# Attention beside a two-layer product on one core: half-array matmuls issued in longer rows, and one PSUM pool of four banks

## The chip, the cores and the metric

The kernel runs on one core of a Trainium2 chip. The metric is the device time of one execution in microseconds; the time before is the median of three runs, 242.66 us (242.25 to 243.97). Everything below that is read from a profile is read from one profiled execution of the kernel before.

## The reference

For each of 4 batches and 8 heads, 768 queries of 64 numbers attend to the keys within 15 places of their own (a band of 31) and, beside them, to one summary per block of 32 tokens: the maximum of the block's keys, with the mean of its values, and log 32 added to the score. The result, 3072 rows of 512, goes through two products with a quick GELU between them.

```python
k_sum = k.reshape(B, H, nb, block, D).max(axis=3)
v_sum = v.reshape(B, H, nb, block, D).mean(axis=3)
mask_l = np.abs(pos[:, None] - pos[None, :]) < window
scores_all = np.concatenate([where(mask_l, scale*q@k.T, -1e9), scale*q@k_sum.T + log(block)], axis=-1)
attn = softmax(scores_all) @ np.concatenate([v, v_sum], axis=2)
h = x @ w_in                      # x: attn as 3072 x 512
out = (h * sigmoid(1.702 * h)) @ w_out
```

## The kernel before

The work is cut into eight **units** u = 0 to 7, half a batch each (384 rows of x). A unit has two stages on TensorE (PE). `ff_in` makes the hidden layer: 16 groups (nt) of four matmuls `ph` of 384 columns, each group followed by a GELU on ScalarE (ACT). `ff_out` makes the output: three row blocks (ms) of 16 matmuls `po` of 512 columns, cut into 12 **slots** of four matmuls each. In u = 0 the slots run over the three blocks in turn, so three `po` tiles are open at once; in the other units one block is done before the next.

The attention of unit u+1 is woven between the slots of unit u, by a table `plan` (L705) that the function `beside` (L708) reads after each slot. For each of four head pairs p it has three steps:

- `s<p>`, `scores` (L470): twelve matmuls `ps_s` of 64 columns that use 64 of the array's 128 rows; then the exponential on ACT and the mask multiply on VectorE (DVE). The first exponential of a unit stands behind a load of ACT's table.
- `v<p>`, `values` (L487): twelve matmuls `ps_av` of 65 columns that use 64 of the array's 128 columns, for the two heads, three query blocks and two halves. Of the 65 columns 64 are the sums and one is the weights' total. `norm` (L501) is a reciprocal and a multiply on DVE and leaves `x_sb`.
- `x<p>`, `tx` (L508): three full-array transposes `ps_x` of `x_sb`, and a DVE copy to `xT[p]`, which the matmul number p of each `ph` group of the next unit reads.

The engines do their instructions in the order in which the program issues them (`_Ordered`, L17, whose helper line L27 all rows of the profile carry). So an instruction that waits holds all that stands behind it on its engine.

When a batch has ended (u = 1, 3 and 5), the next batch's keys, values and queries are prepared within `ff_in`: GpSimd (POOL) casts them; PE transposes keys (`tk`, L454) after groups 1, 2, 4 and 6, block sums of values (`vsum`, L235) after groups 8 and 9, queries (`tq`, L464) after groups 10, 11, 13 and 14. Behind each `tk` stands a chain on DVE: a copy out of PSUM, a maximum `ks` over blocks, and five small copies; behind the second half of `vsum` four small casts `vs`, from which two DMAs on the SP queue fill the summary rows of `vw` (`vrows`, L286) that the first `v` of the next unit reads.

PSUM has eight banks, in three pools: `psb` (two tiles of two banks: scores, values, transposed keys and queries), `psx` (one bank: `ps_x` and the block sums `ps_vs`) and `pmm` (three banks: `ph`, `po`). A tile must wait until the last reader of the earlier tile in its banks is done.

Of the kernel before, what the change touches and what calls it, by code (L numbers as in the profile page):

```python
# [9 lines left out]
F32 = mybir.dt.float32  # L10
BF16 = mybir.dt.bfloat16
# [23 lines left out]
def kernel(  # L35
# [10 lines left out]
    B, H, S, D = q.shape  # L46
# [5 lines left out]
    NP = H // 2  # L52
# [17 lines left out]
    keep = ctx.enter_context(tc.tile_pool(name="keep", bufs=1))  # L70
# [2 lines left out]
    attp = ctx.enter_context(tc.tile_pool(name="att", bufs=4))  # L73
    outp = ctx.enter_context(tc.tile_pool(name="outp", bufs=3))
    psb = ctx.enter_context(tc.tile_pool(name="psb", bufs=2, space=bass.MemoryType.PSUM))
    psx = ctx.enter_context(tc.tile_pool(name="psx", bufs=1, space=bass.MemoryType.PSUM))
    pmm = ctx.enter_context(tc.tile_pool(name="pmm", bufs=3, space=bass.MemoryType.PSUM))

# [88 lines left out]
    vs = keep.tile([128, H, VC], BF16, name="vs")  # L167
    vse = keep.tile([128, H, VC], BF16, name="vse")
    vso = keep.tile([128, H, VC], BF16, name="vso")
    xT = [keep.tile([128, HALF], BF16, name=f"xT{p}") for p in range(NP)]  # L170
    gT = [keep.tile([128, NT, HALF], BF16, name=f"gT{s}") for s in range(2)]
    w_in_sb = keep.tile([128, KO, d_ff], BF16, name="w_in_sb")
    w_out_sb = keep.tile([128, NT, d_model], BF16, name="w_out_sb")
# [59 lines left out]
    vs_ps = [None]  # L233

    def vsum(s, js):  # L235

        if js[0] == 0:
            vs_ps[0] = psx.tile([128, 2 * D], F32, name="ps_vs", tag="x")
        w5 = vw[s].rearrange("p (j e) h c -> p j e h c", e=2)
        for j in js:  # L240
            o = 20 - 4 * j
            for g in range(4):
                pe.matmul(out=vs_ps[0][32 * g:32 * g + 32, :], lhsT=E[:, o:o + 32],
                          rhs=w5[:, j, 0, 2 * g:2 * g + 2, 0:D],
                          start=(j == 0), stop=(j == NJ - 1), skip_group_check=True)
# [132 lines left out]
    def v_sum(j):  # L378

        if j == 0:  # L380
            st["VS"] = psx.tile([128, H * D], F32, name="ps_vs", tag="x")
# [46 lines left out]

    def x_turn(p):
        src = x_sb.pop(p)  # L430
        pool_, tag = (psx, "x") if st["nx"] % 2 == 0 else (pmm, "mm")
        st["nx"] += 1
        st["X", p] = pool_.tile([128, HALF], BF16, name="ps_x", tag=tag)
# [36 lines left out]
    def scores(b, half, p):  # L470

        a = a_sb[p] = attp.tile([128, 2, TH, QT], BF16, name="a_sb", tag="a_sb")
        big = psb.tile([128, 1024], F32, name="ps_s", tag="big")
        for i in range(TH):
            t = half * TH + i
            for h in range(2):
                r = slice(h * 64, h * 64 + 64)
                pe.matmul(out=big[:, h * 512 + i * QT:h * 512 + i * QT + QT],
                          lhsT=kx[p][b % 2][r, t, :], rhs=qT[p][r, t * QT:t * QT + QT],
                          start=True, stop=True)  # L480
        act.activation(out=a.rearrange("p h t c -> p h (t c)"),
                       in_=big.rearrange("p (h c) -> p h c", h=2)[:, :, 0:HALF],
                       func=ACT.Exp, scale=scale)
        dve.tensor_mul(a, a, mk[:, half * TH:(half + 1) * TH, :].unsqueeze(1)
                       .to_broadcast([128, 2, TH, QT]))

    def values(b, half, p):  # L487

        a = a_sb[p]
        big = psb.tile([128, 1024], F32, name="ps_av", tag="big")  # L490
        pv = big[:, 0:390].rearrange("p (h j c) -> p h j c", h=2, j=JH)
        for hh in range(2):
            for j in range(JH):
                for e in range(2):
                    t = 2 * j + e
                    pe.matmul(out=pv[e * 64:e * 64 + 64, hh, j, :], lhsT=a[:, hh, t, :],
                              rhs=vw[b % 2][:, half * TH + t, 2 * p + hh, 0:D + 1],
                              start=True, stop=True, skip_group_check=True)
        norm(p, pv)

    def norm(p, pv):  # L501
        rc = attp.tile([128, 2, JH, 1], F32, name="rc", tag="rc")
        dve.reciprocal(out=rc, in_=pv[..., D:D + 1])
        x_sb[p] = attp.tile([128, JH, 2, D], BF16, name="x_sb", tag="x_sb")
        dve.tensor_mul(x_sb[p].rearrange("p j h d -> p h j d"), pv[..., 0:D],
                       rc.to_broadcast([128, 2, JH, D]))

    def tx(p, eng=dve):  # L508
        src = x_sb.pop(p)
        ps = psx.tile([128, HALF], BF16, name="ps_x", tag="x")  # L510
        for j in range(JH):
            pe.transpose(out=ps[:, j * 128:(j + 1) * 128],
                         in_=src[:, j].rearrange("p h d -> p (h d)"), identity=ident)
        copy(eng, xT[p], ps)


    def ff_in(u, nt):
# [32 lines left out]
        load_q(0, p, 0)  # L550
    load_v(0)
    hold = consts.tile([16, 16], BF16, name="hold")
    st["npv"] = st["nx"] = 0
    w50 = vw[0].rearrange("p (j e) h c -> p j e h c", e=2)
    for p in range(NP):
        clear_kx(dve, p, 0)
# [143 lines left out]
    for p in range(NP):  # L700
# [7 lines left out]
    def beside(b, half, slot):  # L708
        for what in plan[slot]:
            p = int(what[1])  # L710
            if what[0] == "s":
                scores(b, half, p)
                if p == NP - 1:
                    gelu_soon()
            elif what[0] == "v":
                values(b, half, p)
            else:
                tx(p)

    for u in range(2 * B):  # L720
        b, half = u // 2, u % 2
        todo = {}
        if u == 0:

            for p in range(NP):
                todo[8 + 2 * p] = [lambda p=p: tq0_late(p, 1)]
        elif half == 1 and b + 1 < B:
            s = (b + 1) % 2
            todo = {1: [lambda: tk(0, s)], 2: [lambda: tk(1, s)],
                    4: [lambda: tk(2, s)], 6: [lambda: tk(3, s)],  # L730
                    8: [lambda: vsum(s, (0, 1, 2))],
                    9: [lambda: vsum(s, (3, 4, 5)), lambda: vrows(s)],
                    10: [lambda: tq(0)], 11: [lambda: tq(1)],
                    13: [lambda: tq(2)], 14: [lambda: tq(3)]}
            cast_k(pool, 0)
            cast_k(pool, 1)
            cast_k(pool, 2)
            cast_k(pool, 3)
            for j in range(NJ):
                cast_v(pool, s, j, 0)  # L740
                cast_v(pool, s, j, 1)
            cast_q(pool, 0)
        for nt in range(NT):
            ff_in(u, nt)
            if half == 1 and b + 1 < B:
                if nt == 9:
                    cast_q(pool, 1)
                    cast_q(pool, 2)
                if nt == 11:
                    cast_q(pool, 3)  # L750
            for f in todo.get(nt, ()):
                f()
        nxt = u + 1 < 2 * B
        i = 0
        order = ([(ms, part) for part in range(4) for ms in range(JH)] if u == 0 else
                 [(ms, part) for ms in range(JH) for part in range(4)])
        for ms, part in order:
            ff_out(u, ms, part)
            if nxt:
                beside((u + 1) // 2, (u + 1) % 2, i)  # L760
# [42 lines left out]
```

## Time and profile before

| | us |
|---|---|
| median of three runs | 242.66 |
| the profiled execution | 242.78 |
| its span | 240.8 |
| PE busy (matmuls) | 224.4 |
| weight loads on PE | 124.1 |
| ACT busy | 132.4 |
| DVE busy | 101.7 |
| POOL busy | 66.1 |

A row of the timeline gives the start of a group of like instructions, the time from the first one's start to the last one's end, the engine, the operation with its output and inputs, the shape (rows*columns of the array for PE) and, in brackets, how long the engine was idle before it and what ended that. Matmuls overlap: one lasts 190 to 400 ns from start to end while the next may start after 15 to 220 ns, so distances between starts are what counts on PE. A few matmul records are missing from the trace: a group that shows x3 where the program has four has lost one record. PEld is PE's weight loads.

### The profile page before, as it was taken

The page shows a single profiled execution, that of the slowest core. Times are in us where ns is not written, and L with a number is a line of the kernel's source. Part 1 is how long each engine was busy: PE and PEld are TensorE (multiplying, and loading weights), DVE is VectorE, ACT ScalarE, POOL GpSimd, SP SyncE. Part 2 cuts the span into 40 slices and gives each one's busy share as a digit, 9 for nine tenths or more (in the row PEclk, how much of TensorE's full clock was granted, in tenths as well). Part 3 has the DMA queues.
Part 4 walks back from the last instruction along what each step waited for, and adds up shares of the span by engine and source line. Part 5 has one row for each costly group of instructions (what it writes and reads, how often), then busy time and mean ns, then how long its engine had stood idle before and what let it go on. Part 6 is the DMA issues. An engine that isn't in the chain of part 4 may idle for free.

```text
span 240.8 us, 5262 instructions
## 1 busy us (share of the span) xinstructions
PE 224.4 (93%) x2110; PEld 124.1 (52%) x2133; DVE 101.7 (42%) x285; ACT 132.4 (55%) x225; POOL 66.1 (27%) x134
## 2 busy tenths in 40 slices
PE   7684799999899999999999999999999999999993
PEld 2531666446464555446654555456654565446541
DVE  5873623365963510355935500456924500550000
ACT  3756165555465467654564478545573478357510
POOL 7579900047730004782000015771000000000000
PEclk9999799999999999999999999999999999999999
DMA  6996999999993169995061189993141110111012
GB/s 187 292 186 102 229 236 209 224 219 207 219 247 100 46 149 220 200 230 164 5 111 46 44 194 218 205 233 116 27 88 46 44 44 3 44 46 44 0 46 88
DMA packets 76537, 32.26 MB, mean 134 GB/s; under 512 B 63857, under 2 KB 73441, under 8 KB 76513
## 3 DMA queue, kind: packets, MB, share of 16 engines
q1 hardware_dynamic: 72288, 27.73, 53.5%
q0 software_dynamic: 4224, 4.19, 10.5%
q8 instruction: 17, 0.28, 0.5%
q14 instruction: 8, 0.06, 0.1%
HBM read 27.26 MB, written 6.29 MB: 139 GB/s over the span
## 4 chain that ended last, share of the span: by engine, by line
PE 73%; SPq 10%; DMA 9%; DVE 2%; issue 2%; POOL 1%; ACT 0%; POOLq 0%; ACTq 0%
PE ph L27 31%; PE po L27 30%; SPq L27 10%; PE ps_av L27 4%; DMA qf<-in_q_dram 4%; PE ps_s L27 3%; DMA vw<-vw 2%; PE ps_t L27 2%; PE ps_x L27 2%; DMA kf<-in_k_dram 2%; DMA vw<-vs 1%; DVE ks L27 1%; POOL vw L27 1%; PE ps_vs L27 1%; PE ps_q L27 1%
## 5 line engine op out<-in xcount | busy, mean ns | idle before, releaser
L27 PE MATMUL po<-w_out_sb,gT 128*128 128x512 bf16 x362 | 92.6, 380 | 2.6 <-issue 2.2
L27 PE MATMUL ph<-xT,w_in_sb 128*128 128x384 bf16 x512 | 91.3, 326 | 0.1
L27 ACT ACTIVATE gT<-ph 128x384 bf16<-128x384 f32 x128 | 62.9, 491 | 35.0 <-PE ph L27 35.0
L27 PEld LDWEIGHTS <-w_in_sb 128*128 128x128 bf16 x512 | 48.4, 98 | 29.5 <-issue 1.6
L27 DVE TENSOR_TENSOR a_sb<-a_sb,mk 128x768 bf16<-128x768 bf16 x32 | 19.8, 624 | 67.3 <-ACT a_sb L27 66.5
L27 PEld LDWEIGHTS <-gT 128*128 128x128 bf16 x384 | 32.4, 98 | 30.6
L27 ACT ACTIVATE a_sb<-ps_s 128x768 bf16<-128x768 f32 x32 | 25.1, 809 | 23.9 <-PE ps_s L27 23.8
L27 POOL CAST kb<-kf 128x768 bf16<-128x768 f32 (+1 forms) x15 | 11.5, 768 | 82.5 <-DMA kf<-in_k_dram 49.0
L27 ACT ACTIVATE osb<-po 128x512 f32<-128x512 f32 x24 | 14.2, 593 | 33.5 <-issue 16.9
L27 POOL CAST vw<-vf 128x512 bf16<-128x512 f32 (+2 forms) x45 | 27.4, 651 | 5.2 <-DMA vf<-in_v_dram 5.1
L27 ACT ACT_TABLE_LOAD x16 | 20.5, 1283 | 1.1 <-PEq L787 0.8
L27 PEld LDWEIGHTS <-a_sb 128*64 128x64 bf16 x432 | 10.4, 119 | 17.0 <-issue 10.9
L27 DVE TENSOR_TENSOR x_sb<-ps_av,rc 128x384 bf16<-128x384 f32 x32 | 17.8, 557 | 1.2 <-PE ps_av L27 0.2
L27 PE MATMUL ps_av<-vw,a_sb 128*64 128x65 bf16 x384 | 13.0, 205 | 4.3 <-DMA vw<-vw 4.2
L27 DVE COPY xT<-ps_x 128x384 bf16<-128x384 bf16 x30 | 10.7, 357 | 10.9 <-PE ps_x L27 10.7
L27 POOL CAST qb<-qf 128x768 bf16<-128x768 f32 (+1 forms) x14 | 11.6, 827 | 8.8 <-DMA qf<-in_q_dram 7.4
L27 PEld LDWEIGHTS <-kx 64*128 64x128 bf16 x384 | 7.5, 95 | 11.2 <-issue 9.7
L27 DVE RECIPROCAL rc<-ps_av 128x6 f32<-128x6 f32 x32 | 6.1, 191 | 14.6 <-PE ps_av L27 14.6
L27 PEld LDWEIGHTS <-x_sb 128*128 128x128 bf16 x96 | 7.8, 99 | 7.1 <-DVE x_sb L27 0.2
L27 DVE TENSOR_REDUCE ks<-ps_t 128x24 bf16<-128x768 bf16 x12 | 11.3, 944 | 0.0
L27 PE MATMUL ps_s<-qT,kx 64*128 64x64 bf16 x384 | 11.2, 192 | 0.1
L27 PE MATMUL ps_x<-ident,x_sb 128*128 128x128 bf16 x96 | 10.8, 222 | 0.1
(59 smaller groups left out, 127.2 us busy)
## 6 DMA issues: line engine op xcount, KB each, us to landing
kf<-in_k_dram SPq DMA_DIRECT2D x32, 192.0 KB, 3.9
qf<-in_q_dram SPq DMA_DIRECT2D x32, 192.0 KB, 4.5
vf<-in_v_dram SPq DMA_DIRECT2D x24, 256.0 KB, 5.1
out_dram<-osb SPq DMA_DIRECT2D x24, 256.0 KB, 2.1
w_in_sb<-in_moe_w_in_dram POOLq DMA_DIRECT2D x4, 512.0 KB, 10.6
w_out_sb<-in_moe_w_out_dram POOLq DMA_DIRECT2D x4, 512.0 KB, 18.3
vw<-vs SPq DMA_DIRECT2D x6, 148.5 KB
vw<-vw SPq DMA_DIRECT2D x6, 99.0 KB, 3.1
```

The lines of the kernel that those rows point to most:

```text
L27: r = f(*a, **kw)
```

## The change

Three things, all in PSUM and in the order of PE's work.

**Order.** `values` now takes two head pairs (g is pairs 2g and 2g+1): 24 matmuls, then the two `norm`s. `tx` takes two pairs: six transposes into one bank and one copy of 768 columns to a tile `xTT[g]` that holds both. The plan groups them: both first scores in slot 0, both first values and both last scores in slot 4, transposes in slot 6, values in slot 8, transposes in slot 10. For unit 1, which is woven into u = 0 with its three open `po` tiles, there is a plan of its own with fewer tiles: the last scores in slot 7, the last values in slot 10, the last transposes in slot 11.

**Banks.** `psx` is gone and `pmm` has four banks. The values of a pair go to one bank of `pmm` each; only unit 1's two pairs share a two-bank tile of `psb`, one bank each.

**Block sums.** `ps_vs` of u = 1, 3 and 5 goes to a two-bank tile of `psb`, between the transposed keys and the transposed queries; that of batch 0 goes to `pmm`.

```diff
-    psx = ctx.enter_context(tc.tile_pool(name="psx", bufs=1, space=bass.MemoryType.PSUM))
-    pmm = ctx.enter_context(tc.tile_pool(name="pmm", bufs=3, space=bass.MemoryType.PSUM))
+    pmm = ctx.enter_context(tc.tile_pool(name="pmm", bufs=4, space=bass.MemoryType.PSUM))
...
-    xT = [keep.tile([128, HALF], BF16, name=f"xT{p}") for p in range(NP)]
+    xTT = [keep.tile([128, 2, HALF], BF16, name=f"xT{g}") for g in range(2)]
+    xT = [xTT[p // 2][:, p % 2] for p in range(NP)]
...
-            vs_ps[0] = psx.tile([128, 2 * D], F32, name="ps_vs", tag="x")
+            vs_ps[0] = psb.tile([128, 1024], F32, name="ps_vs", tag="big")[:, 0:2 * D]
...
-    def values(b, half, p):
-
-        a = a_sb[p]
-        big = psb.tile([128, 1024], F32, name="ps_av", tag="big")
-        pv = big[:, 0:390].rearrange("p (h j c) -> p h j c", h=2, j=JH)
-        for hh in range(2):
...
-        norm(p, pv)
+    def values(b, half, g, big):
+
+        ps = psb.tile([128, 1024], F32, name="ps_av", tag="big") if big else None
+        pvs = []
+        for i in range(2):
+            p = 2 * g + i
+            a = a_sb[p]
+            one = (ps[:, i * 512:i * 512 + 512] if big else
+                   pmm.tile([128, 512], F32, name="ps_av", tag="mm"))
+            pv = one[:, 0:390].rearrange("p (h j c) -> p h j c", h=2, j=JH)
+            pvs.append(pv)
+            for hh in range(2):
...
+        for i in range(2):
+            norm(2 * g + i, pvs[i])
...
-    def tx(p, eng=dve):
-        src = x_sb.pop(p)
-        ps = psx.tile([128, HALF], BF16, name="ps_x", tag="x")
-        for j in range(JH):
...
-        copy(eng, xT[p], ps)
+    def tx(g):
+        ps = pmm.tile([128, 2, HALF], BF16, name="ps_x", tag="mm")
+        for i in range(2):
+            src = x_sb.pop(2 * g + i)
+            for j in range(JH):
...
+        dve.tensor_copy(out=xTT[g], in_=ps)
...
-    plan = {0: ["s0"], 1: ["s1"], 2: [], 3: ["v0"], 4: ["s2"], 5: ["v1"], 6: ["x0", "s3"],
-            7: ["v2"], 8: ["x1"], 9: ["v3"], 10: ["x2"], 11: ["x3"]}
+    plan = {0: ["s0", "s1"], 4: ["v0", "s2", "s3"], 6: ["x0"], 8: ["v1"], 10: ["x1"]}
+
+    plan0 = {0: ["s0", "s1"], 4: ["v0", "s2"], 6: ["x0"], 7: ["s3"], 10: ["v1"], 11: ["x1"]}
...
+        for what in (plan0 if u == 1 else plan).get(slot, ()):
```

The first place is PE in u = 2, from slot 0 on, as the program of the kernel before has it (weight loads and like rows left out; numbers tell tiles apart: `ps_s_1583` and `ps_s_1636` are the scores of pairs 0 and 1, `ps_av_1662` and `ps_av_1704` the values of these pairs, `po_1577` and `po_1679` the first two row blocks):

```order
L27 MATMUL po_1577<-w_out_sb_123,gT0_120 128x512
...
L27 MATMUL ps_s_1583<-qT0_107,kx0_1_100 128x64
...
L27 MATMUL ps_s_1636<-qT1_108,kx1_1_102 128x64
...
L27 MATMUL ps_av_1662<-vw1_112,a_sb_1582 64x65
...
L27 MATMUL po_1679<-w_out_sb_123,gT0_120 128x512
...
L27 MATMUL ps_s_1685<-qT2_109,kx2_1_104 128x64
...
L27 MATMUL ps_av_1704<-vw1_112,a_sb_1635 64x65
```

And as the changed program has it:

```order
L27 MATMUL po_1562<-w_out_sb_118,gT0_115 128x512
...
L27 MATMUL ps_s_1568<-qT0_104,kx0_1_97 128x64
...
L27 MATMUL ps_s_1584<-qT1_105,kx1_1_99 128x64
...
L27 MATMUL po_1647<-w_out_sb_118,gT0_115 128x512
...
L27 MATMUL ps_av_1652<-vw1_109,a_sb_1567 64x65
...
L27 MATMUL ps_av_1665<-vw1_109,a_sb_1583 64x65
...
L27 MATMUL ps_s_1687<-qT2_106,kx2_1_101 128x64
...
L27 MATMUL ps_s_1703<-qT3_107,kx3_1_103 128x64
```

In the kernel before, `po` matmuls stand between any two of these groups; now pair 1's scores follow pair 0's directly, and in slot 4 two pairs of values and two pairs of scores follow one another with nothing between.

The second place is PE at the end of u = 0, where the last attention step of unit 1 leads into the next `ff_in`. Before (`a_sb_926` is pair 3's weights, `x_sb_962` and `x_sb_995` are what `norm` left for pairs 2 and 3):

```order
L27 MATMUL ps_av_980<-vw0_111,a_sb_926 64x65
...
L27 MATMUL po_829<-w_out_sb_123,gT0_120 128x512
...
L27 MATMUL ps_x_1004<-ident_82,x_sb_962 128x128
...
L27 MATMUL po_850<-w_out_sb_123,gT0_120 128x512
...
L27 MATMUL ps_x_1016<-ident_82,x_sb_995 128x128
...
L27 MATMUL ph_1043<-xT3_119,w_in_sb_122 128x384
```

Now:

```order
L27 MATMUL ps_av_962<-vw0_108,a_sb_891 64x65
...
L27 MATMUL ps_av_962<-vw0_108,a_sb_927 64x65
...
L27 MATMUL po_845<-w_out_sb_118,gT0_115 128x512
...
L27 MATMUL ps_x_1002<-ident_79,x_sb_989 128x128
...
L27 MATMUL ps_x_1002<-ident_79,x_sb_993 128x128
...
L27 MATMUL ph_1032<-xT1_114,w_in_sb_117 128x384
```

The values of pairs 2 and 3 now stand one slot (four `po`) ahead of their transposes, where pair 3's stood two slots ahead; the third matmul of the first `ph` group reads the copy of these transposes (`xT1_114` holds pairs 2 and 3).

The third place is PE in the `ff_in` of u = 1, where the block sums begin. Before, with the waits:

```order
L27 MATMUL ps_t_1127<-ident_82,kb_1027 128x128 [waits PE_49]
...
L27 MATMUL ph_1147<-xT3_119,w_in_sb_122 128x384
L27 LDWEIGHTS E_87
L27 MATMUL ps_vs_1153<-vw1_112,E_87 32x128 [waits Pool_49]
...
L27 MATMUL ps_t_1220<-ident_82,qb_1172 128x128 [waits PE_49]
```

Now:

```order
L27 MATMUL ps_t_1116<-ident_79,kb_1016 128x128 [waits PE_49]
...
L27 MATMUL ph_1136<-xT1_114,w_in_sb_117 128x384
L27 LDWEIGHTS E_84 [waits DVE_49,PE_49]
L27 MATMUL ps_vs_1142<-vw1_109,E_84 32x128 [waits Pool_49]
...
L27 MATMUL ps_t_1209<-ident_79,qb_1161 128x128 [waits PE_49]
```

The order is the same, but the first weight load of the block sums now has a wait for DVE: their two-bank tile takes the place of the third key transpose, which is free once its maximum `ks` is done. The query transposes that follow have moved on by one tile: the second of them (`ps_t_1209`) now has the banks of the block sums, and is free to start once the four casts `vs` are done.

More of the change, by code (lines that the diff above doesn't have):

```diff
@@ L380, in v_sum @@
         if j == 0:
-            st["VS"] = psx.tile([128, H * D], F32, name="ps_vs", tag="x")
+            st["VS"] = pmm.tile([128, H * D], F32, name="ps_vs", tag="mm")
             st["VT"] = pmm.tile([128, H * D], F32, name="ps_vt", tag="mm")
@@ L430, in x_turn @@
         src = x_sb.pop(p)
-        pool_, tag = (psx, "x") if st["nx"] % 2 == 0 else (pmm, "mm")
-        st["nx"] += 1
-        st["X", p] = pool_.tile([128, HALF], BF16, name="ps_x", tag=tag)
+        st["X", p] = pmm.tile([128, HALF], BF16, name="ps_x", tag="mm")
         for j in range(JH):
@@ L485, in scores @@
                        .to_broadcast([128, 2, TH, QT]))
-    def values(b, half, p):
-        a = a_sb[p]
-        big = psb.tile([128, 1024], F32, name="ps_av", tag="big")
-        pv = big[:, 0:390].rearrange("p (h j c) -> p h j c", h=2, j=JH)
-        for hh in range(2):
-            for j in range(JH):
[L494 to L498, printed above, removed]
-        norm(p, pv)
+    def values(b, half, g, big):
[10 more added lines that the diff above has]
+                for j in range(JH):
+                    for e in range(2):
+                        t = 2 * j + e
+                        pe.matmul(out=pv[e * 64:e * 64 + 64, hh, j, :], lhsT=a[:, hh, t, :],
+                                  rhs=vw[b % 2][:, half * TH + t, 2 * p + hh, 0:D + 1],
+                                  start=True, stop=True, skip_group_check=True)
+        for i in range(2):
+            norm(2 * g + i, pvs[i])
     def norm(p, pv):
@@ L506, in norm @@
                        rc.to_broadcast([128, 2, JH, D]))
-    def tx(p, eng=dve):
-        src = x_sb.pop(p)
-        ps = psx.tile([128, HALF], BF16, name="ps_x", tag="x")
-        for j in range(JH):
-            pe.transpose(out=ps[:, j * 128:(j + 1) * 128],
-                         in_=src[:, j].rearrange("p h d -> p (h d)"), identity=ident)
-        copy(eng, xT[p], ps)
+    def tx(g):
+        ps = pmm.tile([128, 2, HALF], BF16, name="ps_x", tag="mm")
+        for i in range(2):
+            src = x_sb.pop(2 * g + i)
+            for j in range(JH):
+                pe.transpose(out=ps[:, i, j * 128:(j + 1) * 128],
+                             in_=src[:, j].rearrange("p h d -> p (h d)"), identity=ident)
+        dve.tensor_copy(out=xTT[g], in_=ps)
     def ff_in(u, nt):
@@ L552 @@
     hold = consts.tile([16, 16], BF16, name="hold")
-    st["npv"] = st["nx"] = 0
+    st["npv"] = 0
     w50 = vw[0].rearrange("p (j e) h c -> p j e h c", e=2)
@@ L702, with beside @@
     clear_vw(pool, 1)
-    plan = {0: ["s0"], 1: ["s1"], 2: [], 3: ["v0"], 4: ["s2"], 5: ["v1"], 6: ["x0", "s3"],
-            7: ["v2"], 8: ["x1"], 9: ["v3"], 10: ["x2"], 11: ["x3"]}
-    def beside(b, half, slot):
-        for what in plan[slot]:
-            p = int(what[1])
+    plan = {0: ["s0", "s1"], 4: ["v0", "s2", "s3"], 6: ["x0"], 8: ["v1"], 10: ["x1"]}
+    plan0 = {0: ["s0", "s1"], 4: ["v0", "s2"], 6: ["x0"], 7: ["s3"], 10: ["v1"], 11: ["x1"]}
+    def beside(u, slot):
+        b, half = u // 2, u % 2
+        for what in (plan0 if u == 1 else plan).get(slot, ()):
+            i = int(what[1])
             if what[0] == "s":
-                scores(b, half, p)
-                if p == NP - 1:
+                scores(b, half, i)
+                if i == NP - 1:
                     gelu_soon()
             elif what[0] == "v":
-                values(b, half, p)
+                values(b, half, i, u == 1)
             else:
-                tx(p)
+                tx(i)
     for u in range(2 * B):
@@ L759 @@
             if nxt:
-                beside((u + 1) // 2, (u + 1) % 2, i)
+                beside(u + 1, i)
             i += 1
```

## The prediction

> **What bounds the kernel now.** I read the page first, then the waits of PE, then PE's timeline from start to start.
>
> ```profile
> PE 224.4 (93%) x2110; PEld 124.1 (52%) x2133; DVE 101.7 (42%) x285; ACT 132.4 (55%) x225; POOL 66.1 (27%) x134
> PE   7684799999899999999999999999999999999993
> PE 73%; SPq 10%; DMA 9%; DVE 2%; issue 2%; POOL 1%; ACT 0%; POOLq 0%; ACTq 0%
> ```
>
> ```profile
> PE ps_av L27 <- DMA vw<-vw: 4.2, 1, 4.2
> PE ps_t L27 <- DVE ks L27: 0.8, 1, 0.8
> ```
>
> From the sixth slice on PE is at 8 or 9 in every slice but the last, and the chain that ended last is mostly PE's. The waits of PE that count are few: 4.2 us once, before the first unit, in a part whose order the change leaves as it is, and 0.8 us once. So only a shorter stream on PE, or small waits that this view does not name, can pay. "Busy" cannot show what a change of the array's shape costs, since a matmul counts as busy until its modelled end; distances between starts can:
>
> ```profile
> 84.29 1.03 PE L27 MATMUL po<-w_out_sb,gT 128*128 128x512 bf16 x4
> 85.16 0.33 PE L27 MATMUL ps_x<-ident,x_sb 128*128 128x128 bf16 x3
> 85.32 10.68 PE L27 MATMUL ph<-xT,w_in_sb 128*128 128x384 bf16 x64
> 95.84 1.03 PE L27 MATMUL po<-w_out_sb,gT 128*128 128x512 bf16 x3
> 96.80 0.35 PE L27 MATMUL ps_s<-qT,kx 64*128 64x64 bf16 x12
> 97.08 1.04 PE L27 MATMUL po<-w_out_sb,gT 128*128 128x512 bf16 x4
> 98.05 0.35 PE L27 MATMUL ps_s<-qT,kx 64*128 64x64 bf16 x12
> 98.33 1.90 PE L27 MATMUL po<-w_out_sb,gT 128*128 128x512 bf16 x8
> 100.16 0.38 PE L27 MATMUL ps_av<-vw,a_sb 128*64 128x65 bf16 x12
> ...
> 110.09 1.58 PE L27 MATMUL ph<-xT,w_in_sb 128*128 128x384 bf16 x8
> ```
>
> ```profile
> L27 PE MATMUL ps_av<-vw,a_sb 128*64 128x65 bf16 x384 | 13.0, 205 | 4.3 <-DMA vw<-vw 4.2
> L27 PE MATMUL ps_s<-qT,kx 64*128 64x64 bf16 x384 | 11.2, 192 | 0.1
> ```
>
> Four `po` before transposes take 85.16 - 84.29 = 0.87, so one takes 0.216 to 0.218; three transposes take 0.16 to 0.17. Between `po` and scores it is different. 97.08 to 98.05 is 0.97, that is 0.11 more than four `po` (4 x 0.216 = 0.86). The twelve scores last 0.35 with one of them lasting 0.19, so the last starts 0.16 after the first and a thirteenth could start at 0.175; but `po` resumes at 98.33, 0.28 after 98.05: 0.11 more again. So each entry into a half-array shape and each return costs about 0.11 us in which nothing streams. The whole `ff_out` of u = 2 says the same: 110.09 - 95.84 = 14.25, less 12 x 0.863 for `po` and 4 x 0.167 for transposes leaves 3.2 for eight half-array groups, 0.40 each. Twelve scores stream in 0.175 and twelve values in 0.38 - 0.20 + 0.015 = 0.19, so 0.22 of the 0.40 is two changes.
>
> Does a second twelve, with other weights and another bank, pay anything? One place has values of different tiles in a row, at half the clock:
>
> ```profile
> 26.45 0.24 PE L27 MATMUL ps_av<-vso,a_sb 128*64 128x64 bf16 x1
> 26.46 0.57 PE L27 MATMUL ps_av<-vw,a_sb 128*64 128x65 bf16 x12
> 26.84 0.21 PE L27 MATMUL ps_av<-vse,a_sb 128*64 128x64 bf16 x1
> ```
>
> Twelve in 0.38 and 0.01 between the tiles: nothing at the seam.
>
> **The change, part by part.** *Grouping.* Before, a unit pays 16 changes of shape (eight groups, in and out). In the plan of units 2 to 7, slots 0, 4 and 8 pay 2 + 3 + 2 = 7, if the step from values to scores within slot 4 costs one change. Nine times 0.11 is 1.0 us for each of six units. In unit 1, slots 0, 4, 7 and 10 pay 2 + 3 + 2 + 2 = 9: 0.77 less. No row has the step from values to scores. Its bounds are nothing (as at the seam above) and 0.22 (as if through the full array); I take 0.11, the row of one change, and the bounds are worth 7 x 0.11 = 0.8 us either way. The Trainium skill, TensorEngine Tiling (Array Packing), Key Properties, says that a change of tiling mode drains TensorE while a change of tile does not; by it this step pays one drain and the sum stays; with no drain it would be 0.8 lower.
>
> *Transposes.* Six in a row cost PE what two times three did. What matters is the copy behind them.
>
> ```profile
> 83.36 0.20 DVE L27 RECIPROCAL rc<-ps_av 128x6 f32<-128x6 f32 x1 [0.82 <-PE ps_av L27]
> 83.59 0.56 DVE L27 TENSOR_TENSOR x_sb<-ps_av,rc 128x384 bf16<-128x384 f32 x1
> 85.52 0.36 DVE L27 COPY xT<-ps_x 128x384 bf16<-128x384 bf16 x1 [0.67 <-PE ps_x L27]
> 85.94 0.58 PEld L27 LDWEIGHTS <-w_in_sb 128*128 128x128 bf16 x4 [0.19 <-issue]
> L27 DVE COPY qT<-ps_t 128x768 bf16<-128x768 bf16 x12 | 6.6, 556 | 4.0 <-PE ps_t L27 3.7
> ```
>
> Pair 3's copy ends at 85.88, and the fourth `ph` matmul, due at 85.32 + 3 x 0.163 = 85.81 (95.84 - 85.32 is 10.52 for 64, less this loss), gets its weights at 85.94: 0.13 lost at the head of every `ff_in`. In units 2 to 7 the last transposes move to slot 10. The copy of 768 columns (0.556, as for `qT`) starts 0.25 after the last transpose starts (85.16 + 0.11 to 85.52) and has reached PE at 0.86, with 0.05 for the way (85.88 to 85.94); the third `ph` matmul is due at 0.06 + 0.86 (slot 11) + 0.33 = 1.25. Hidden, and 0.13 saved six times. Without slot 11 as cover it would cost 0.48, as at the end of u = 0 below.
>
> *Norms and masks in the steady units.* Two norms in a row take 2 x (0.23 + 0.56) = 1.58 on DVE, from 0.24 after the first pair's last matmul (82.94 + 0.18 to 83.36); that matmul is 0.19 ahead of the second pair's. So both `x_sb` have reached PE 0.24 + 1.58 + 0.05 - 0.19 = 1.68 after the last values matmul. PE returns (0.13), runs two slots (1.73) and three transposes (0.17): it asks for the second at 2.03. Spare 0.35. At slot 6 the scores of slot 4 lie between as well, 0.46 more. The bank of the fourth pair's values is the one that slot 6's transposes had. These end 2.8 after the first pair's last values matmul; on DVE two norms and two masks stand ahead of their copy (0.24 + 1.58 + 2 x 0.56 = 2.9), which is done at 3.6, and the values come at 4.8. The masks of the first two scores:
>
> ```profile
> 98.69 1.44 DVE L27 TENSOR_TENSOR a_sb<-a_sb,mk 128x768 bf16<-128x768 bf16 x2 [12.81 <-ACT a_sb L27]
> ```
>
> The exponentials there follow ACT's table load, not the scores, so the masks end at 100.13 as before. The values of slot 4 start at 96.80 + 0.35 + 0.11 + 16 x 0.216 + 0.11 = 100.8. Spare 0.7.
>
> *The end of u = 0.* Here one slot, not two, lies between the last values and their transposes, both pairs share one tile, so the first reciprocal waits for all 24 matmuls. Pair 3's `x_sb` is there 0.24 + 1.58 + 0.05 = 1.87 after the last; PE wants it at 0.13 + 0.87 + 0.17 = 1.17: 0.70 lost. Then the copy (0.86 after the last transpose starts) holds the third `ph` matmul, due at 0.38: 0.48 lost. 1.18, less the 0.13 paid before and the 0.77 saved: `ff_in` of u = 1 starts its second group 0.28 **later**.
>
> *Block sums in `psb`.* They now wait for the third key transpose's maximum, and the second query transpose for the four casts:
>
> ```profile
> 63.86 0.94 DVE L27 TENSOR_REDUCE ks<-ps_t 128x24 bf16<-128x768 bf16 x1
> 64.23 0.35 PE L27 MATMUL ps_vs<-vw,E 128*32 128x128 bf16 x12
> 66.91 1.18 DVE L27 CAST vs<-ps_vs 32x128 bf16<-32x128 f32 x4
> 67.19 0.50 PE L27 MATMUL ps_t<-ident,qb 128*128 128x128 bf16 x6
> 72.10 3.27 DMA vw<-vs
> 75.12 0.66 PE L27 MATMUL ps_av<-vw,a_sb 128*64 128x65 bf16 x12
> ```
>
> In u = 1 DVE is behind: that maximum ends at 64.80, but PE starts the sums at 64.23; the casts end at 68.09, but the query transpose starts at 67.19. With DVE's chain 0.15 to 0.25 later, the sums start at 65.0 (0.77 late), the transpose at 68.26 (1.07 late). Nothing after it recovers this: slot 0 of u = 1 starts 1.07 late. Then a gain: the first values of u = 2 wait 0.28 (0.66 against 0.38) for the summary rows, which land at 75.37. The chain to them is the SP queue, the loads and POOL's casts, which the change moves nowhere; the values now come at about 76.9, one slot further on, and do not wait.
>
> In u = 3 (and 5) the same pair of waits does not bite:
>
> ```profile
> 116.04 0.95 DVE L27 TENSOR_REDUCE ks<-ps_t 128x24 bf16<-128x768 bf16 x1
> 117.49 0.35 PE L27 MATMUL ps_vs<-vw,E 128*32 128x128 bf16 x12
> 119.10 1.17 DVE L27 CAST vs<-ps_vs 32x128 bf16<-32x128 f32 x4
> 120.46 0.50 PE L27 MATMUL ps_t<-ident,qb 128*128 128x128 bf16 x6
> ```
>
> Spare 0.5 and 0.19.
>
> **The sum.** Six units times (1.0 + 0.13) is 6.8 less; the DMA wait 0.3 less; u = 0 and the `ff_in` of u = 1 together 1.07 more: 6.0 less than the profiled execution's 242.78, or **236.8 us** (span 234.8). The profiled execution is 0.1 above the median of 242.66, so against the median it is a little under 6 too.
>
> **Rivals.** *The u = 1 waits are hidden* (chance 0.10): if DVE's chain keeps up, the 1.07 turns into the 0.77 saved, and the time is about 235.0. Against it: the rows above have DVE behind already.
>
> *Waits in every unit* (0.10): DVE stands on the way to slots 6, 8 and 10, and if its norms stretch by a fifth when POOL casts beside them, the 1.58 grows by 0.3 and the spare of 0.35 is nearly gone; if each of six units then loses 0.3 to 0.5, 238.6 to 239.8. Against it, least, median and most of the norm's multiply:
>
> ```profile
> L27 DVE TENSOR_TENSOR x_sb<-ps_av,rc x32: 556/557/559, 26.7 to 214.3; 128x384 bf16<-128x384 f32 x32
> ```
>
> It never stretches, beside POOL or not.
>
> *The price goes with each twelve, not with the change of shape* (0.04): new weights and a new bank at a group's start cost the 0.22, grouped or not. Then only 6 x 0.13 + 0.3 = 1.1 is saved, u = 0 loses 1.05 and the `ff_in` of u = 1 0.8: 243.5, **slower than before**. It decides when a change of shape is worth under 0.012 us (61 changes fewer against a net loss of 0.75). The seam at 26.46 speaks against it.
>
> *The clock* (0.02): a pool of four banks that all stages turn through, with new small waits, could bring PE's granted clock down.
>
> ```profile
> 20.00:30.00 10.00, 5.74 (x115) 4.10 (x114) 4.56 (x13) 3.10 (x6) 9.60 (x34) 0.83 1.05 188
> 60.00:70.00 10.00, 9.19 (x99) 5.73 (x97) 9.63 (x27) 4.91 (x10) 6.50 (x10) 1.00 1.28 254
> ```
>
> The seventh column after the window's length is the clock: the 4.2 us wait cost 0.17 x 10 = 1.7 us of it; the 0.8 us wait at 62 us cost none. One such loss in each of seven units would be 12 us: 248.7. The longest new wait I find is 0.8 us. The Trainium skill, TensorE: Matmul & The Clock Gate, A second HAM failure mode, tells of a kernel whose turning through PSUM banks did swing the clock; no run here shows it.
>
> **How the numbers follow.** The forecast has 0.74; its own range is 235.9 to 237.8 (0.8 for the step from values to scores, some tenths for u = 1). To leave no more than 2 in 10 out it must reach down to 235.0 and into the waits in every unit: 235.0 to 238.8. About 1% can be told from no change by a measurement of this kernel, so faster means under 240.2: 0.74 + 0.10 + 0.10, less 0.04 for what I have not seen, 0.90; within 1% 0.07 (the price with each twelve, 0.04, and most of that doubt); slower 0.03 (the clock, and the rest).
>
> **What would show it.** Right: one gap of about 0.1 where values pass to scores in slot 4 and none between two pairs; no stop at the head of `ff_in` from u = 2 on; a stop of some 0.7 before the last three transposes of u = 0 and of 0.5 in the `ph` group behind them; block sums in u = 1 that wait for `ks`; an `ff_out` of about 13.2 us (14.25 less 1.0) from its first `po` to the first `ph`. Wrong: PE waits at slots 6, 8 or 10 in u = 2 to 6, a clock under 1.00 after 30 us, or gaps of 0.2 between two pairs.

## The result, and the profile after

The changed kernel takes 237.11 us (median of 4 runs, 236.72 to 237.67), the kernel before 242.71 beside it (242.25 to 243.97): 0.9763 of the time, 95% interval 0.9727 to 0.9798. Run again on another chip it took 236.85 (236.50 to 237.33) against 242.59: 0.9766 (0.9747 to 0.9784). The forecast was 236.8. The profiled execution of the changed kernel took 237.29 us, with a span of 235.2.

The page of the changed kernel, busy time by engine and PE's slices:

```profile
PE 220.5 (94%) x2133; PEld 124.5 (53%) x2133; DVE 98.4 (42%) x271; ACT 132.4 (56%) x225; POOL 66.3 (28%) x134
PE   7794699998989999999999999999999999999993
```

PE's busy time fell by 3.9 us with no matmul fewer in the program, and its share rose: most of what went is time that counted as busy, since a matmul is booked until its modelled end. The view that shows it is PE's timeline. One `ff_out` of the changed kernel, u = 2, with start, length and what was run:

```profile
85.42 10.56 PE L27 MATMUL ph<-xT,w_in_sb 128*128 128x384 bf16 x64
95.83 1.03 PE L27 MATMUL po<-w_out_sb,gT 128*128 128x512 bf16 x4
96.78 0.52 PE L27 MATMUL ps_s<-qT,kx 64*128 64x64 bf16 x24
97.24 3.63 PE L27 MATMUL po<-w_out_sb,gT 128*128 128x512 bf16 x16
100.80 0.57 PE L27 MATMUL ps_av<-vw,a_sb 128*64 128x65 bf16 x24
101.30 0.52 PE L27 MATMUL ps_s<-qT,kx 64*128 64x64 bf16 x24
101.75 1.90 PE L27 MATMUL po<-w_out_sb,gT 128*128 128x512 bf16 x8
...
109.08 1.14 PE L27 MATMUL ph<-xT,w_in_sb 128*128 128x384 bf16 x6
```

From the first `po` to the first `ph` it is 109.08 - 95.83 = 13.25 us, where it was 14.25. Values to scores in slot 4 take 101.30 - 100.80 = 0.50; twenty-four values stream in 0.39 (the last starts 0.57 - 0.20 = 0.37 after the first), so 0.11 is left: one change of shape. Two pairs of scores last 0.52 where one lasted 0.35, that is 0.17 more, just the second twelve: nothing at the seam. `ff_in` takes 95.83 - 85.42 = 10.41 (10.52 before), and no row from 85.42 to 109.08 has a wait.

The waits of PE in the changed kernel that are new or bear on this (us in all, times, longest), and its timeline where u = 0 ends and u = 1 prepares the second batch:

```profile
PE ps_vs L27 <- DVE ks L27: 0.6, 1, 0.6
PE ps_x L27 <- DVE x_sb L27: 0.6, 2, 0.4
PE ps_t L27 <- DVE ks L27: 0.5, 1, 0.5
...
PE ph L27 <- DVE xT L27: 0.3, 1, 0.3
```

```profile
55.33 0.34 PE L27 MATMUL ps_x<-ident,x_sb 128*128 128x128 bf16 x3
56.02 0.34 PE L27 MATMUL ps_x<-ident,x_sb 128*128 128x128 bf16 x3 [0.35 <-DVE x_sb L27]
56.20 0.49 PE L27 MATMUL ph<-xT,w_in_sb 128*128 128x384 bf16 x2
57.01 1.14 PE L27 MATMUL ph<-xT,w_in_sb 128*128 128x384 bf16 x6 [0.32 <-DVE xT L27]
...
65.28 0.35 PE L27 MATMUL ps_vs<-vw,E 128*32 128x128 bf16 x12 [0.59 <-DVE ks L27]
...
68.56 0.50 PE L27 MATMUL ps_t<-ident,qb 128*128 128x128 bf16 x6 [0.16 <-POOL qb L27]
...
72.17 1.03 PE L27 MATMUL po<-w_out_sb,gT 128*128 128x512 bf16 x4
```

The bracket counts only the time after the last matmul's modelled end; starts tell what is lost. Three transposes start a fourth 0.17 later, but here 56.02 - 55.33 = 0.69: 0.52 lost (and 0.08 in front of the first three). Two `ph` take 0.33, but 57.01 - 56.20 = 0.81: 0.48 lost. u = 1 reaches its slot 0 at 72.17, where the kernel before had 70.80; u = 0 had its own slot 0 at 42.11 against 41.61, so 0.87 of the 1.37 was lost between the two. The rows of the kernel before:

```profile
41.61 1.03 PE L27 MATMUL po<-w_out_sb,gT 128*128 128x512 bf16 x3
...
70.80 1.03 PE L27 MATMUL po<-w_out_sb,gT 128*128 128x512 bf16 x3
```

The row at 68.56 names the query's cast, but that cast had ended at 65.93 + 0.83 = 66.76. The four casts `vs` end at 67.25 + 1.17 = 68.42, and in the five other profiles whose program is the same up to here the wait is put down to `vs`. So the second query transposes wait for the banks of the block sums, as the program's order has it.

### The profile page after: what moved, and what is told of

It is laid out like the page before. It is cut to its first block, busy times and chain, and to the rows that moved or that the text cites. A ratio compares the mean times of both kernels' runs of the same rounds, so it can differ in the third digit from the quotient of the medians.

```text
span 235.2 us, 5274 instructions
## 1 busy us (share of the span) xinstructions
PE 220.5 (94%) x2133; PEld 124.5 (53%) x2133; DVE 98.4 (42%) x271; ACT 132.4 (56%) x225; POOL 66.3 (28%) x134
## 4 chain that ended last, share of the span: by engine, by line
PE 76%; SPq 11%; DMA 8%; issue 1%; ACT 1%; DVE 0%; POOL 0%; ACTq 0%; POOLq 0%
PE ph L27 32%; PE po L27 32%; SPq L27 11%; PE ps_av L27 4%; PE ps_t L27 3%; DMA vf<-in_v_dram 3%; PE ps_s L27 2%; DMA vw<-vw 2%; PE ps_x L27 2%; DMA qf<-in_q_dram 2%; DMA kf<-in_k_dram 2%; PE ps_vs L27 1%; PE ps_q L27 1%; POOL qb L27 0%; PE ps_w L27 0%
## 5 line engine op out<-in xcount | busy, mean ns | idle before, releaser
L27 PE MATMUL po<-w_out_sb,gT 128*128 128x512 bf16 x384 | 90.1, 380 | 0.0
L27 PEld LDWEIGHTS <-gT 128*128 128x128 bf16 x384 | 35.2, 98 | 37.2
L27 ACT ACTIVATE a_sb<-ps_s 128x768 bf16<-128x768 f32 x32 | 24.4, 808 | 12.6 <-PE ps_s L27 12.6
L27 PEld LDWEIGHTS <-a_sb 128*64 128x64 bf16 x432 | 9.4, 120 | 11.8 <-issue 11.8
L27 PE MATMUL ps_av<-vw,a_sb 128*64 128x65 bf16 x384 | 10.1, 203 | 5.1 <-DMA vw<-vw 5.1
L27 DVE COPY xT<-ps_x 128x768 bf16<-128x768 bf16 (+1 forms) x16 | 8.5, 531 | 7.3 <-PE ps_x L27 7.3
L27 PEld LDWEIGHTS <-kb 128*128 128x128 bf16 x120 | 7.7, 107 | 5.5 <-POOL kb L27 1.9
L27 PE MATMUL ps_w<-warm 128*128 128x512 bf16 x25 | 8.9, 461 | 1.4 <-DVE warm L27 1.3
L27 PE MATMUL ps_x<-ident,x_sb 128*128 128x128 bf16 x96 | 8.5, 222 | 0.6 <-DVE x_sb L27 0.6
```

The costliest lines, as they stand in the source:

```text
L27: r = f(*a, **kw)
```

## The experiments

All are the changed kernel with the edit shown, but one, which starts from the kernel before. "Stage P" is the way from slot 0 of u = 0 to slot 0 of u = 1 (first `po` to first `po`), which holds all the stops shown above.

**More changes of shape.** Three kernels undo the grouping of units 2 to 7 in steps and leave banks, joint transposes and unit 1 alone.

```diff
-plan = {0: ["s0", "s1"], 4: ["v0", "s2", "s3"], 6: ["x0"], 8: ["v1"], 10: ["x1"]}
+plan = {0: ["s0", "s1"], 4: ["v0"], 5: ["s2", "s3"], 6: ["x0"], 8: ["v1"], 10: ["x1"]}                 # one
+plan = {0: ["s0"], 1: ["s1"], 4: ["v0", "s2"], 5: ["s3"], 6: ["x0"], 8: ["v1"], 10: ["x1"]}            # four
+plan = {0: ["s0"], 1: ["s1"], 3: ["w0"], 4: ["s2"], 5: ["w1"], 6: ["s3"], 7: ["x0", "w2"], 8: ["w3"], 10: ["x1"]}  # nine; w: values of one pair
```

> The changed kernel with the scores of pairs 2 and 3 moved from slot 4 to slot 5, behind one more set of four po, in units 2 to 7: 8 changes of array shape a unit instead of 7. If each change costs 0.11 us, 6 x 0.11 = 0.66 us more than the changed kernel's 237.1, 237.8. If the price goes with each twelve matmuls, or the step from values to scores cost nothing at the seam, two other numbers: 0 more (237.1) with the price on each twelve; 6 x 0.22 = 1.3 more (238.4) if the step inside slot 4 had been free.

> The changed kernel with the scores of the four pairs in slots 0, 1, 4 and 5, one pair each, and the values still two pairs together, in units 2 to 7: 11 changes of array shape a unit instead of 7. Price by change: 6 x 4 x 0.11 = 2.6 us more than the changed kernel, 239.7. Price by twelve: nothing more, 237.1.

> The changed kernel with every pair's scores and values in a group by itself (slots 0, 1, 3, 4, 5, 6, 7, 8) in units 2 to 7, banks and joint transposes as in the change: 16 changes of array shape a unit, as before the change. Price by change: 6 x 9 x 0.11 = 5.9 us more, 243.0, slightly above the kernel before since u = 0 and u = 1 keep their losses and the 0.13 a unit is kept. Price by twelve: nothing more, 237.1, and the gain lies in banks and transposes.

| kernel | changes in a unit | `ff_out` of u = 2, us | median, us | of the kernel before (95%) |
|---|---|---|---|---|
| changed, second time | 7 | 13.26 | 236.85 | 0.9766 (0.9747 to 0.9784) |
| one more | 8 | 13.37 | 237.45 | 0.9789 (0.9765 to 0.9813) |
| four more | 11 | 13.69 | 239.39 | 0.9866 (0.9843 to 0.9888) |
| nine more | 16 | 14.25 | 242.89 | 1.0006 (0.9992 to 1.0020) |

The third kernel's u = 2 on PE, from its first `po` and first twelve scores to its first `ph`:

```profile
96.17 1.03 PE L27 MATMUL po<-w_out_sb,gT 128*128 128x512 bf16 x3
97.13 0.35 PE L27 MATMUL ps_s<-qT,kx 64*128 64x64 bf16 x12
...
110.42 0.81 PE L27 MATMUL ph<-xT,w_in_sb 128*128 128x384 bf16 x4
```

110.42 - 96.17 is 14.25, what it was before the change. The stage grows on a line: 0.11, 0.43 and 0.99 us for one, four and nine changes, 0.11 each, and the time with it: 0.6, 2.4 and 5.8 us by the ratios (each less 0.9766, times 242.6), 0.7, 2.6 and 5.9 by six units. The 0.6 of the first step is within the noise of the times (the intervals overlap); the stage tells it, 13.37 against 13.26 in the profiles. A price on each twelve would have left all three at 237.1. With the grouping alone undone, the whole gain is gone. The first step shows the seam too: parting values and scores costs 0.11 and neither nothing nor 0.22, so inside slot 4 one change is paid. By the Trainium skill, TensorEngine Tiling (Array Packing), Key Properties, a change of tiling mode drains TensorE and a change of tile does not; these rows agree, the step from one half-array shape to the other included. What the rows show is the price of a change, not what the engine does in the gap.

**One piece alone, from the other side.** The kernel before with only the first scores joined, in all seven units.

```diff
-plan = {0: ["s0"], 1: ["s1"], 2: [], ...
+plan = {0: ["s0", "s1"], 1: [], 2: [], ...
```

> The kernel before with one piece of the change alone: the scores of pairs 0 and 1 both in slot 0, in all seven units; pools and all else as before. Price by change of shape: two changes fewer in each of seven units, 7 x 0.22 = 1.5 us less than 242.7, 241.1. Price by twelve, or a gain that needs the merged pool: 242.7.

241.49 us against 243.07 beside it, 0.9944 (0.9921 to 0.9967): 1.4 us less. Six of the seven `ff_out` are 0.21 shorter (14.24 to 14.03), for two changes; that of u = 1, where the first values wait for the summary rows, kept its 14.52. The price holds without the merged pool.

**The cover of the last transposes.** Slot 11 instead of 10.

```diff
-... 8: ["v1"], 10: ["x1"]}
+... 8: ["v1"], 11: ["x1"]}
```

> The changed kernel with the last transposes of units 2 to 7 in slot 11 instead of slot 10: no po lies between them and the ph of the next unit. My working: the joint copy of 768 columns then holds the third ph matmul by 0.48 us (as at the end of u = 0, 0.487 in the trace), for six units 2.9 us more, 240.0. If the loss at the end of u = 0 came from something of that stage alone: no more, 237.1.

239.66 us, 0.9878 (0.9853 to 0.9904), 2.7 us more than the changed kernel by the ratios (0.9766). PE at the end of its u = 2, and its wait over the whole run:

```profile
109.90 0.50 PE L27 MATMUL ps_x<-ident,x_sb 128*128 128x128 bf16 x6
110.24 0.49 PE L27 MATMUL ph<-xT,w_in_sb 128*128 128x384 bf16 x2
111.05 1.14 PE L27 MATMUL ph<-xT,w_in_sb 128*128 128x384 bf16 x6 [0.32 <-DVE xT L27]
```

```profile
PE ph L27 <- DVE xT L27: 2.3, 7, 0.3
```

The third `ph` comes at 0.81, not 0.33: 0.48 lost, in each of seven units now, one of which had it already. The four `po` of slot 11 are what hides the joint copy.

**Unit 1's two stops.** One kernel puts the later block sums into a bank of the pool of four, one moves unit 1's steps forward, one does both.

```diff
-            vs_ps[0] = psb.tile([128, 1024], F32, name="ps_vs", tag="big")[:, 0:2 * D]
+            vs_ps[0] = pmm.tile([128, 2 * D], F32, name="ps_vs", tag="mm")
...
-plan0 = {0: ["s0", "s1"], 4: ["v0", "s2"], 6: ["x0"], 7: ["s3"], 10: ["v1"], 11: ["x1"]}
+plan0 = {0: ["s0", "s1"], 4: ["v0", "s2"], 6: ["x0", "s3"], 8: ["v1"], 10: ["x1"]}
```

> The changed kernel with the block sums of the later batches in a single bank of the pool of four instead of psb. My theory: the stop before them in the ff_in of u = 1 (0.75 us lost) and the one before the second query transpose (0.32, a wait for the casts of the sums through the shared bank, not for the cast of the query that the trace names) both go: 1.07 less than the changed kernel's 237.1, 236.0. Rival: VectorE's chain of casts and copies sets the end of this ff_in anyway, and the waits only move to a later transpose: 237.1, at best 0.3 less. If the second stop is the query's cast, 0.75 less: 236.4.

> The changed kernel with unit 1's steps one or two slots earlier: the last scores in slot 6, the second two pairs' values in slot 8, their transposes in slot 10, as in the other units (9 changes of shape still). My theory: the 0.60 us lost before the last three transposes and the 0.49 in the ph group behind them both go, 1.1 less than 237.1, 236.0, and VectorE's chain in u = 1 starts as much earlier. Rival: the gain is swallowed by the waits for VectorE and DMAs in the ff_in of u = 1 (0.65, 0.75 and 0.32 lost now): 237.1. If the mask of pair 3 comes too late for slot 8, a new stop of some tenths there.

> Both edits in one: block sums in a single bank of the pool of four, and unit 1's steps one or two slots earlier. If the two losses add, 1.07 + 1.09 = 2.2 less than the changed kernel: 234.9. If the second only feeds waits that the first leaves, no more than the better of the two alone, about 236.0.

The first was run a second time, beside the changed kernel on one chip:

> The changed kernel itself, beside the one with the sums in the pool of four on the same chip. If its head (first ph at 30.11 in its profile, against 27.5 to 30.6 in the others that share its code up to there) is only an execution's chance, the ratio to the kernel before is 0.974 to 0.978 and the first ph comes between 28.9 and 30.6; if the change itself delays the head by 0.5 us, the first ph is again at 30 or later.

> The kernel with the block sums in the pool of four a second time. If the two stops of u = 1 (0.75 and 0.32) are all that it removes, it is 1.1 us under the changed kernel run beside it; if, as its first profile has it, slot 0 of u = 1 comes at the time that the loads and casts set (70.4, the fourth query's cast at 69.3) whatever the head does, 1.2 to 1.9 under it, and slot 0 of u = 1 is at 70.2 to 70.6 again.

| kernel | slot 0 of u = 0 | slot 0 of u = 1 | stage P | median, us | of the kernel before (95%) |
|---|---|---|---|---|---|
| before | 41.61 | 70.80 | 29.19 | 242.71 | |
| changed | 42.11 | 72.17 | 30.06 | 237.11 | 0.9763 (0.9727 to 0.9798) |
| changed, second time | 40.85 | 71.49 | 30.64 | 236.85 | 0.9766 (0.9747 to 0.9784) |
| sums in the pool of four | 40.50 | 70.37 | 29.87 | 235.56 | 0.9689 (0.9662 to 0.9716) |
| the same, second time | 41.60 | 71.01 | 29.41 | 236.25 | 0.9743 (0.9716 to 0.9771) |
| unit 1's steps earlier | 41.90 | 71.67 | 29.77 | 236.36 | 0.9731 (0.9695 to 0.9767) |
| both | 41.22 | 70.37 | 29.15 | 235.68 | 0.9697 (0.9670 to 0.9725) |

The `ff_in` of u = 1 on PE, first of the kernel with the sums in the pool of four, then of the one with both edits:

```profile
63.12 0.35 PE L27 MATMUL ps_vs<-vw,E 128*32 128x128 bf16 x12
...
66.09 0.50 PE L27 MATMUL ps_t<-ident,qb 128*128 128x128 bf16 x6
...
67.49 0.82 PE L27 MATMUL ph<-xT,w_in_sb 128*128 128x384 bf16 x4 [0.26 <-DVE vs L27]
...
69.37 0.51 PE L27 MATMUL ps_t<-ident,qb 128*128 128x128 bf16 x6
...
70.37 1.03 PE L27 MATMUL po<-w_out_sb,gT 128*128 128x512 bf16 x3
```

```profile
53.50 0.50 PE L27 MATMUL ps_x<-ident,x_sb 128*128 128x128 bf16 x6
...
54.70 1.46 PE L27 MATMUL ph<-xT,w_in_sb 128*128 128x384 bf16 x8
...
66.08 0.51 PE L27 MATMUL ps_t<-ident,qb 128*128 128x128 bf16 x6 [0.53 <-POOL qb L27]
...
67.55 0.82 PE L27 MATMUL ph<-xT,w_in_sb 128*128 128x384 bf16 x4 [0.31 <-DVE vs L27]
...
69.38 0.51 PE L27 MATMUL ps_t<-ident,qb 128*128 128x128 bf16 x6
...
70.37 1.03 PE L27 MATMUL po<-w_out_sb,gT 128*128 128x512 bf16 x3
```

POOL's casts of the second and the fourth query in the kernel with both edits:

```profile
65.20 0.83 POOL L27 CAST qb<-qf 128x768 bf16<-128x768 f32 x1 [0.97 <-DMA qf<-in_q_dram]
...
68.49 0.83 POOL L27 CAST qb<-qf 128x768 bf16<-128x768 f32 x1 [0.66 <-DMA qf<-in_q_dram]
```

The stop before the sums goes in both. The second query transposes run without a wait in the first kernel (66.09), which agrees with the reading that the banks held them. With both edits the sums come earlier still, and the same transposes stop for something else: 0.53 us for their query's cast, whose row (65.20 + 0.83 = 66.03) ends just before them. With unit 1's steps moved, six transposes and eight `ph` run through.

But the gains do not add: 1.07 and 1.09 were expected, and the kernel with both has a stage P of 29.15, 0.9 to 1.5 shorter than the changed kernel's two. Its 235.68 us is near the 236.0 that was expected if the second edit only feeds waits that the first leaves. Moving unit 1's steps alone saved 1.07 at the end of u = 0 and lost some of it again: its `ff_in` of u = 1, without the stop of 0.48, still took 16.27 us, where the changed kernel's two took 15.97 and 16.54 with it. The loss stands in front of the fourth key transposes, which wait for DVE's maximum `ks` behind the second ones: 0.49 and 0.42 us in the changed kernel's two profiles and 1.28 here.

```profile
62.40 0.49 PE L27 MATMUL ps_t<-ident,kb 128*128 128x128 bf16 x6 [1.28 <-DVE ks L27]
```

The two kernels with the sums moved whose u = 0 began at 40.50 and 41.22 reach slot 0 of u = 1 at the same 70.37. In both POOL's cast of the fourth query ends at 68.49 + 0.83 = 69.32, after a wait for its load, and the last query transposes start 0.05 to 0.06 later (69.37 and 69.38). PE itself would have come to them about 0.2 us earlier (four `ph` of 0.163 after 68.49 and 68.54), so in these two executions the load and cast of the fourth query set the end of the stage. In the second profile of the kernel with the sums moved they do not: that cast ends at 69.80, but PE gets to the transposes only at 70.03, behind a wait of 0.66 for the maximum `ks` in front of the fourth key transposes, and slot 0 comes at 71.01. This second run was 0.6 us under the changed kernel beside it, where 1.1 or 1.2 to 1.9 had been expected with slot 0 at 70.2 to 70.6: neither came. Part of the wait has moved as well: in the two kernels shown, the `ph` whose turn comes to the sums' bank now waits for their casts.

**Loads earlier.** Both edits, and the small transfer that holds back the second batch's loads waits for an earlier step of `ff_in`.

```diff
-    sp.dma_start(out=hold, in_=gT[0][0:16, NT - 1, 0:16])
+    sp.dma_start(out=hold, in_=gT[0][0:16, NT - 3, 0:16])    # the other: NT - 6
```

> The kernel with both edits, and the loads of the second batch's keys, values and queries released two ff_in steps of u = 0 earlier (the small transfer in front of them waits for step 13's result instead of step 15's). My theory: what now ends the ff_in of u = 1 is the stream of loads and their casts on GpSimd (the fourth query's cast ends at 69.32, its transpose starts at 69.37, slot 0 at 70.37 in both kernels with the sums in the pool of four). Then slot 0 of u = 1 comes up to 1.5 us earlier and 0.7 to 1.3 are saved: 234.4 to 235.0. Rival: VectorE's own chain of copies and maxima sets it, or the loads only take the bandwidth from the weights of the second product, which then come late in u = 0: 235.7 or more.

> The same with the loads released five steps earlier. If loads and casts are what ends that stage: as the kernel with two steps or up to 0.5 less, 234.0 to 234.6, until no stop is left but those for VectorE. If the weights of the second product come late: a stop of PE in the ff_out of u = 0, and 235.7 or more.

235.91 us, 0.9706 (0.9681 to 0.9731), and 236.14, 0.9730 (0.9708 to 0.9752): no gain on the 0.9697 of both edits alone. Slot 0 of u = 1 comes at 70.73 and 71.03, after starts of u = 0 at 42.08 and 41.50: a stage P of 28.65 and 29.53, one shorter and one longer than the 29.15 without it, by no more than two executions of one program differ above (30.06 and 30.64). The SP queue's issue of the keys' loads with both edits alone, then with the loads released five steps earlier, and POOL's first cast of the new batch in the latter:

```profile
42.59 7.90 SPq L27 DMA_DIRECT2D kf<-in_k_dram  x8
```

```profile
38.64 12.54 SPq L27 DMA_DIRECT2D kf<-in_k_dram  x8
```

```profile
49.47 0.82 POOL L27 CAST kb<-kf 128x768 bf16<-128x768 f32 x1 [19.60 <-DMA kf<-in_k_dram]
```

The issue of the keys' loads begins 3.95 us earlier and takes 4.6 us longer. The first cast starts at 49.47 where it had been 49.00, and the fourth query's cast ends at 69.98 (69.53 with two steps) where it had been 69.32: neither came earlier. My theory that an earlier release brings the loads earlier fell; so did its rival's late weights, since no stop of PE appears in the `ff_out` of u = 0. The transfers already run at a rate that an earlier release does not raise: 224 GB/s from 26 to 42 us in either kernel, and from 42 to 56 us 222 without it and 214 with it. That these bytes set the floor is argued from the rates, not shown by taking bytes away.

## Why the prediction was right

*The price of a change of shape* (nine changes, 1.0 us, for each of six units): 14.25 to 13.25 in the profile, and 0.11 for each change in the three steps. The value 0.11 for values to scores, which I had chosen between 0 and 0.22, was right.

*The head of `ff_in`* (0.13 for each unit): 0.11 to 0.12. Its condition, slot 11 as cover, was shown by taking the cover away: 0.48 a unit, as worked out.

*Norms and masks in the steady units*: no wait at slots 4, 6, 8 or 10, as said.

*The summary rows* (0.28 no longer waited for): the `ff_out` of u = 1 fell by 1.27 us, from 14.52 to 13.25; 1.0 + 0.28 was the working.

*The end of u = 0* (stops of 0.70 and 0.48): 0.60 and 0.48, at the places named.

*The `ff_in` of u = 1* (slot 0 later by 1.07, waits for `ks` and for the casts): the places were right. The size is the loosest term: stage P was 0.87 longer than before in the first profile of the change, and 1.1 to 1.6 longer in five others whose program is the same up to there (30.29 to 30.75 against 29.19). I had let DVE's chain run 0.15 to 0.25 later and otherwise as before. Counted from slot 0 of u = 0, its casts `vs` start 0.16 earlier than before in the first profile and 0.08 to 0.53 later in the five others: it has no fixed length, as the next section but one shows.

*The sum*: 6.0 less was forecast, 5.5 less stands between the two profiled executions and 5.6 and 5.7 between the medians. The difference in the profiles is the head: u = 0 starts 0.50 later. The wait for the DMA within `vw` ahead of the first values (5.13 against 4.20) and what follows it did that,

```profile
25.77 0.77 PE L27 MATMUL ps_av<-vw,a_sb 128*64 128x65 bf16 x21 [5.13 <-DMA vw<-vw]
...
30.11 6.30 PE L27 MATMUL ph<-xT,w_in_sb 128*128 128x384 bf16 x36
42.11 0.59 PE L27 MATMUL po<-w_out_sb,gT 128*128 128x512 bf16 x2
```

and it is an execution's chance: the same kernel's second profile has no such stop, its `ph` start at 25.14 (earlier even than the 28.9 to 30.6 that had been expected if it is chance) and its slot 0 comes at 40.85, after two waits for the weights.

```profile
21.29 0.72 PE L27 MATMUL ps_av<-vw,a_sb 128*64 128x65 bf16 x24
...
25.14 3.05 PE L27 MATMUL ph<-xT,w_in_sb 128*128 128x384 bf16 x16
30.22 2.77 PE L27 MATMUL ph<-xT,w_in_sb 128*128 128x384 bf16 x16 [2.03 <-DMA w_in_sb<-in_moe_w_in_dram]
...
40.85 1.03 PE L27 MATMUL po<-w_out_sb,gT 128*128 128x512 bf16 x3
```

So a start 1.26 us earlier came out 0.7 us earlier at slot 0 of u = 1 (71.49 against 72.17): the rest is taken back in stage P, and a difference of some tenths between two single profiles says little about a change. Stage P is on the average of the six profiles 1.29 longer than in the one profile of the kernel before, 0.22 more than the forecast's 1.07, which would be most of what the medians fall short of 6.0. That one median came within 0.05 us of 236.8 is partly luck.

*The rivals*: hidden waits in u = 1, the price with each twelve and waits in every unit are refuted by the rows above; the granted clock was 1.00 in every 10 us from 30 to 230 us. In the prediction's rows the clock is the sixth column after the window's length, not the seventh.

## What to carry to other kernels

Count the changes of array shape on PE, not the small groups: in the gaps between starts (never in busy time) each cost 0.11 us here, and work of one shape from different tiles could be put in a row for nothing, as long as every reader behind it keeps a slot of other work as cover. Then look at the one stage where other engines are already behind: there a shared pair of banks added two stops, and what their removal paid did not follow from their length, since other chains stood right behind. Putting the block sums into the pool of four gave the lowest time of the study, 0.9689 and 0.9743 of the time before in two tries against 0.9763 and 0.9766 for the change; side by side on one chip the gain of that edit, 0.6 us, is not clear of the noise (0.9716 to 0.9771 against 0.9747 to 0.9784).

## What the runs showed of the hardware

DVE's copies between places in SBUF stretch while POOL casts; those that read PSUM do not. The rows of the changed kernel, least, median and most in ns:

```profile
L27 DVE COPY kx<-kx x45: 161/172/621, 8.3 to 168.5; 128x80 bf16<-128x80 bf16 x30, 128x192 bf16<-128x192 bf16 x15
L27 DVE COPY kx<-ps_t x12: 541/550/558, 58.5 to 167.0; 128x768 bf16<-128x768 bf16 x12
```

In the `ff_in` of u = 1 three such copies take 0.98 us while POOL casts values, and 0.36 where it is idle:

```profile
59.86 0.98 DVE L27 COPY kx<-kx 128x80 bf16<-128x80 bf16 x3
...
65.05 0.36 DVE L27 COPY kx<-kx 128x80 bf16<-128x80 bf16 x3
```

```profile
59.02 4.58 POOL L27 CAST vw<-vf 128x512 bf16<-128x512 f32 x8 [0.88 <-DMA vf<-in_v_dram]
64.13 0.83 POOL L27 CAST qb<-qf 128x768 bf16<-128x768 f32 x1 [0.54 <-DMA qf<-in_q_dram]
```

In other profiles the first three took from 0.79 to 1.76 us. These copies stand in the chain that stage P hangs on, so it has no fixed length; the longest, 1.76, stands in the kernel with unit 1's steps earlier, ahead of its wait of 1.28. The prediction had asked whether DVE stretches beside POOL, but looked only at the norm's multiply, which reads PSUM. The Trainium skill, SBUF — State Buffer, Who interferes with whom, says that copies can enter a mode in which they contend for the port pair that VectorE shares with GpSimd, and that on trn2 reductions never contend. The rows agree: the maxima `ks` of the changed kernel take 940 to 949 ns wherever they stand. That the casts cause the stretch was not tried by moving them.

The granted clock from 20 to 30 us differed between executions of one program: 0.83 in the changed kernel's first profile, 1.00 in its second, where the 5 us stop was missing.
